# A forward transform folded twice over d in a fused spectral filter and MLP

## The chip, the cores and the metric

One core of a Trainium2 chip runs the kernel. The metric is device time in microseconds of one execution. The engines are TensorE (PE, matrix products; its weight loads are listed as PEld), VectorE (DVE), ScalarE (ACT), GpSimd (POOL) and SyncE (SP), whose queue issues most transfers.

## The reference

```python
def reference(A_x, A_w_r, A_w_i, B_x, B_w1, B_b1, B_w2, B_b2, gate_w):
    ...
        X = (lambda x, axes=(-2,-1): jnp.fft.rfft2(x, axes=axes))(x, axes=(-2, -1))
        W = w_r + 1j * w_i
        X = X * W
        y = (lambda x, s, axes=(-2,-1): jnp.fft.irfft2(x, s=s, axes=axes))(X, (S, D), axes=(-2, -1))
    ...
        h = jnp.einsum("bsd,df->bsf", x, w1) + b1
        h = _gelu(h)
        return jnp.einsum("bsf,fd->bsd", h, w2) + b2
    x = A_x
    g = _sigmoid((x * gate_w).sum(-1, keepdims=True))
    a = _A_ref(x, A_w_r, A_w_i)
    b = _B_ref(x, B_w1, B_b1, B_w2, B_b2)
    return g * a + (1 - g) * b
```

There are S = 2048 tokens of D = 512 elements and F = 1792 hidden units, all float32. Every token is Fourier transformed over d (257 frequencies remain) and the sequence over its 2048 positions, the result is multiplied by a complex filter and transformed back. An MLP with gelu works on the same tokens, and a gate per token mixes both.

## The kernel before

**Precision.** Products run on float32r operands, which keep 12 bits of mantissa here. So each operand x is split into h (ScalarE copies x into a float32r tile) and l = x - h (VectorE), and a full product is made of three: h times h, l times h, h times l. Tables are split on the host.

**Tiling.** Token s is 16a + j: 16 groups j of 128 tokens a. `forward(j)` (L546) transforms group j. It loads the group as four parts of 128 rows of d, folds the parts once (L551: `eo` is the sum and the difference of the upper and the lower half), splits `eo` into h and l, and multiplies with the table `cft` of cosines and sines into `pd` (one half for each of real and imaginary part, c = 0, 1). `high` (L569) makes eight products of 258 columns, two parts q, two values of c and the table's h and l; `low` (L575) makes four with the low part of the tokens. The 258 columns are 257 frequencies and one for the gate's logit. The second part of the table is made on the chip by copying and negating the first (L489 to L503). From `pd` ScalarE makes the high part `x{j}h`, VectorE the low part `x{j}l` and the logit; six products with the table `tf` transform over the 128 tokens (`py`), and L609 to L621 bring the two results into `Y[j]`: for the groups in `BY_ACT` with one VectorE instruction and two half-height ScalarE copies, for the first four groups with two half-height VectorE instructions.

After the forward transforms VectorE works through the rest of the sequence transform: `stage1`, a correction of two rows that goes through memory (`own_rows`), `filt`, `stage4`, and `inverse(c, h)`, which needs TensorE again (`pz`, `pa`).

**The MLP.** The hidden units come in two halves of seven tiles of 128, the tokens in four blocks c of 512. `mlp(half, c)` (L895) makes for each hidden tile f an up-projection of 12 products of 512 columns (`ph`), gelu on ScalarE, the split into `g` (h on ScalarE, l on VectorE), and then for four output tiles q down-projections of three products per hidden tile (`po`). The block's tokens are the pair `X[half, c]`; for block 0 they are split from the groups that the forward transform loads anyway, for the others `load_mx` (L532) loads and splits four groups, and `keep_x` (L524) stores the pair to memory for the second half. `load_w` (L884) loads a weight tile and splits it; for the second half the low part is made by `minus` (L447): ScalarE writes -h, and an accumulating transfer issued by POOL adds x from memory.

**What sets the order.** The functions only register steps with an engine, a modelled cost, a rank and the buffers they read and write. `Graph.schedule` (L211) simulates the engines and issues, on each engine, the ready step of the lowest rank whose buffers are to be had; a step waits for a slot of its buffer's tag (`slots`, L348, with limits for single classes in `most`, L352). The real engines then keep that order. Ranks: 0 for the transform's steps behind `pd`, `EARLY` 0.5, `FEED` 1 for the folds and most splits, `BULK` 5 for the stages behind the forward transform.

Of the kernel before, what the change touches and what calls it, by code (L numbers as in the profile page):

```python
# [14 lines left out]
ALU = mybir.AluOpType  # L15
# [11 lines left out]
CW = 272  # L27


FORD = np.concatenate([np.arange(0, HD, 2), np.arange(1, HD, 2), [HD]])  # L30
# [23 lines left out]
def _tables():  # L54

    d = np.arange(P)[:, None] + 0.5
    f = np.arange(NE)[None, :]
    th = 2 * np.pi * f * d / D
    cf = np.stack([np.cos(th), -np.sin(th)])
    cf[0][:, HD:] = 0.0  # L60
    cf[1][:, 0] = 0.0
    cf[1][:, HD + 1:] = 0.0
    cf = cf[:, :, FORD]

    cf = np.stack(_split(cf[:, :, :ND])).transpose(1, 2, 0, 3)
    cf = np.concatenate([cf, np.zeros((2, P, 2, CW - ND), np.float32)], 3)
# [8 lines left out]
    ])  # L75
# [89 lines left out]
class Graph:  # L165
# [45 lines left out]
    def schedule(self):  # L211
# [45 lines left out]
        while True:  # L257
            for e in list(ready):
                while ready[e] and busy.get(e, 0.0) <= now:
# [37 lines left out]
                    own = [q for q in s.after if q.eng == e == "pe"]  # L297
                    if own:
                        s.after = [q for q in s.after if q.eng != "pe"]
                        n += 1  # L300
                        heapq.heappush(events, (busy[e], n, own))
# [33 lines left out]
def tile_kernel(ctx: ExitStack, tc: tile.TileContext, xt, w1, w2, b1, b2, x0g, wf, wrev, out, consts):  # L335
# [15 lines left out]
    whole = ("xr", "wra", "wrb", "e2", "z", "ttab", "xhl", "wa", "wb", "hid", "so", "ba", "ctab", "gb")  # L351
    most = {("pm", "ph"): 2, ("pm", "po"): 2, ("pm", "po0"): 1, ("pm", "py"): 3, ("t2k", "pq"): 2}  # L352
# [11 lines left out]
    FEED, BULK, EARLY = 1, 5, 0.5  # L364

# [23 lines left out]
    def acc(dst, src, kb, reads, writes, rank=FEED):  # L389

        return add("pool", 2 * kb / 340, 3.6, lambda: nc.gpsimd.dma_start(dst(), src(), accum_op=ALU.add), reads, writes, rank)  # L391
# [19 lines left out]
    gs = one("gs", [P, 2, 2], parts=2)  # L411

    cft = buf("ctab", [P, 2, 2, 2, CW], F32R, "cf", parts=12)
    cfp = {(0, 0): (0,), (1, 0): (1,), (0, 1): (2, 3, 4), (1, 1): (5, 6, 7)}

    def cf(c, q):
        return cft.ap()[:, c, q]

    def cf_of(*cq):
        return [(cft, p) for k in cq for p in cfp[k]] + [(cft, g) for g in range(8, 12)]  # L420
# [7 lines left out]
    gb = one("gb", [P, 4, 4 * P], parts=4)  # L428
# [24 lines left out]
    def load_x(j, tag):  # L453
        x = buf("xr", [P, NQ, P], F32, f"x{tag}{j}")
        dma(lambda: sp.dma_start(x.ap(), xt[j]), 256, [], [x], j / 100 if tag == "f" and j in NORD[:4] else FEED)
        return x
# [14 lines left out]
    x0 = buf("z", [P, NQ + 1, P], F32, "xf0")  # L471
    XF = {0: x0}
    dma_act(lambda: act.dma_start(x0.ap().rearrange("p a b -> p (a b)")[:, :NQ * P + NQ], x0g), 258, [], [x0])
    for j in NORD[1:4]:
        XF[j] = load_x(j, "f")
    for c in range(2):
        dma(lambda c=c: raw(cf(c, 0), cf_d[c]), 272, [], [(cft, k) for k in (c, 8 + c, 10 + c)], 0.6)
# [5 lines left out]
    for k, op in enumerate((ALU.add, ALU.subtract)):  # L483
        tiny(lambda k=k, op=op: vec.tensor_tensor(gs.ap()[:, k], x0.ap()[:, NQ, 0:2], x0.ap()[:, NQ, 2:4], op=op), [x0],
             [(gs, k)])
    gcol = [lambda k=k: cft.ap()[:, :, :, k, NE - 1] for k in range(2)]
    tiny(lambda: vec.tensor_copy(gcol[0](), gs.ap()), [gs], [(cft, 8), (cft, 9)])
    tiny(lambda: vec.tensor_tensor(gcol[1](), gs.ap(), gcol[0](), op=ALU.subtract), [gs, (cft, 8), (cft, 9)], [(cft, 10), (cft, 11)])
    for c in range(2):  # L489
# [602 lines left out]
```

## Time and profile before

| | before |
|---|---|
| median of 3 runs | 380.79 us (380.64 to 381.64) |
| the profiled execution's own time | 381.64 us |
| its span, first to last instruction | 379.6 us |
| HBM read, written | 40.73 MB, 16.92 MB |

The profile's page gives for each engine the time in which it was busy and the number of its instructions. Rows of groups read: line, engine, operation, output<-input with shapes, count, then busy microseconds and mean nanoseconds of one, then the idle time before them and what ended it. Rows of the timeline read: start, length, engine, line, operation; where a row stands for several instructions, its length runs from the first start to the last end. Records of adjacent instructions on one engine overlap at their ends.

### The profile page before, as it was taken

How to read it: one execution, taken by the hardware profiler on the slowest of the kernel's cores; microseconds unless marked ns; L12 is line 12 of the kernel's file. 1: busy time of each engine (PE TensorE's matmuls, PEld its weight loads, DVE VectorE, ACT ScalarE, POOL GpSimd, SP SyncE). 2: the span in 40 equal slices, each digit the busy share in tenths (PEclk: the TensorE clock that was granted, in tenths of full speed). 3: DMA queues.
4: the chain of work that ended last, by engine and by line, in shares of the span. 5: the costliest groups of instructions: out<-in, count | busy, mean ns of one | idle time of the engine just before them, and what ended most of it. 6: DMA issues, size and time to landing. Idle time of an engine off the chain costs nothing.

```text
span 379.6 us, 5546 instructions
## 1 busy us (share of the span) xinstructions
PE 374.2 (99%) x1903; PEld 319.2 (84%) x1903; DVE 324.8 (86%) x683; ACT 220.7 (58%) x385; POOL 19.6 (5%) x26
## 2 busy tenths in 40 slices
PE   8999999989999999999999999999999999999996
PEld 7889999878888888888888888888888888888886
DVE  4999999879797999999999677967799799998732
ACT  6967678947622452288159984398429995134400
POOL 0000000000000000023022001100010000000000
PEclk9999999999999999999999999999999999999999
DMA  8975569895198006179568535413431129623031
GB/s 283 335 229 193 160 228 301 261 329 163 48 289 264 32 28 166 57 185 249 127 170 205 138 148 96 57 35 140 131 38 25 35 88 316 204 82 110 1 112 55
DMA packets 45172, 58.02 MB, mean 153 GB/s; under 512 B 4208, under 2 KB 27312, under 8 KB 44368
## 3 DMA queue, kind: packets, MB, share of 16 engines
q1 hardware_dynamic: 41832, 51.63, 41.9%
q0 software_dynamic: 3168, 5.77, 10.0%
q8 instruction: 15, 0.25, 0.3%
q10 hardware_dynamic: 144, 0.26, 0.2%
q14 instruction: 13, 0.11, 0.1%
HBM read 40.73 MB, written 16.92 MB: 152 GB/s over the span
## 4 chain that ended last, share of the span: by engine, by line
PE 94%; DMA 2%; ACT 1%; DVE 1%; issue 0%; SPq 0%
PE ph L400 40%; PE po L400 38%; PE pd L400 5%; PE pz L400 4%; PE pa L400 3%; PE py L400 3%; DMA wf<-in_wf 2%; PE none L400 1%; ACT y L616 0%; ACT pys L609 0%; SPq L397 0%; DVE pys L613 0%; ACT mxh L520 0%; DVE mxl L521 0%; ACT o L966 0%
## 5 line engine op out<-in xcount | busy, mean ns | idle before, releaser
L929 ACT ACTIVATE ph<-ph,b1t 128x512 f32<-128x512 f32 x56 | 37.0, 661 | 36.9 <-PE ph L400 36.4
L966 ACT ACTIVATE o<-po,b2t 128x512 f32<-128x512 f32 x16 | 11.1, 691 | 36.4 <-PE po L400 35.0
L801 ACT ACTIVATE sw<-y,al 64x512 f32<-64x512 f32 x32 | 23.2, 726 | 2.3 <-DVE y L664 1.6
L760 DVE TENSOR_TENSOR m<-y,wf 128x514 f32<-128x514 f32 x32 | 21.2, 692 | 0.1
L400 PE MATMUL pd<-cf,eoh 128*128 128x258 f32 x128 | 17.8, 282 | 0.0
L400 PEld LDWEIGHTS pd<-cf,eoh 128*128 128x128 f32 x128 | 16.8, 190 | 0.4
L808 DVE SCALAR_TENSOR_TENSOR pq<-y,al,sw 128x256 f32<-128x256 f32 x32 | 14.3, 481 | 1.4 <-ACT sw L804 1.4
L794 ACT ACTIVATE tg<-ti 128x128 fp32r<-128x128 f32 x16 | 5.0, 312 | 15.5 <-DVE ti L792 14.0
L986 DVE TENSOR_TENSOR o<-y,po 128x256 f32<-128x256 f32 x8 | 3.1, 419 | 10.8 <-PE po L400 10.8
L552 DVE TENSOR_TENSOR eo<-xf 128x256 f32<-128x256 f32 x32 | 12.3, 420 | 0.0
L391 POOL DMA_DIRECT2D bacc<-o x8 | 7.0, 873 | 97.2 <-ACT o L969 97.2
L559 DVE TENSOR_TENSOR eol<-eo,eoh 128x512 fp32r<-128x512 f32 (+1 forms) x17 | 11.0, 654 | 0.2
L616 ACT ACTIVATE y<-pys 64x257 f32<-64x257 f32 x24 | 10.1, 420 | 1.9 <-DVE pys L613 1.6
L557 ACT ACTIVATE eoh<-eo 128x512 fp32r<-128x512 f32 (+1 forms) x17 | 10.1, 603 | 1.5 <-DVE eo L552 1.5
L804 ACT ACTIVATE sw<-y 1x512 f32<-1x512 f32 x16 | 10.1, 631 | 0.4
L969 ACT ACTIVATE o<-po 128x512 f32<-128x512 f32 x8 | 4.8, 601 | 9.4 <-PE po L400 5.2
L400 PE MATMUL pd<-cf,eol 128*128 128x258 f32 x64 | 10.1, 283 | 0.0
L391 POOL DMA_DIRECT2D wa7l<-in_w x1 | 1.0, 1017 | 163.1 <-PE ph L400 163.1
L400 PEld LDWEIGHTS pd<-cf,eol 128*128 128x128 f32 x64 | 8.9, 190 | 0.3
L609 ACT ACTIVATE pys<-py 128x257 f32<-128x257 f32 x16 | 6.2, 386 | 5.0 <-PE py L400 4.6
L860 DVE TENSOR_TENSOR u<-pa,od 128x512 f32<-128x512 f32 x8 | 5.5, 690 | 3.4 <-ACT od L850 3.2
L521 DVE TENSOR_TENSOR mxl<-xm,mxh 128x512 fp32r<-128x512 f32 x12 | 7.9, 687 | 0.5 <-ACT mxh L520 0.4
(688 smaller groups left out, 1322.0 us busy)
## 6 DMA issues: line engine op xcount, KB each, us to landing
wf<-in_wf SPq DMA_DIRECT2D x16, 257.0 KB, 4.1
tf<-tf SPq DMA_DIRECT2D x16, 256.0 KB, 3.1
bacc<-o SPq DMA_DIRECT2D x16, 256.0 KB, 3.5
xf<-in_xt SPq DMA_DIRECT2D x15, 256.0 KB, 2.7
war<-in_w SPq DMA_DIRECT2D x14, 256.0 KB, 4.0
wbr<-in_w SPq DMA_DIRECT2D x14, 256.0 KB, 3.3
xm<-in_xt SPq DMA_DIRECT2D x12, 256.0 KB, 4.1
bb<-bacc SPq DMA_DIRECT2D x8, 256.0 KB, 4.0
```

The source lines that it names most:

```text
L391: return add("pool", 2 * kb / 340, 3.6, lambda: nc.gpsimd.dma_start(dst(), src(), accum_op=ALU.add), reads, writes, rank)
L400: pe.matmul(ps, w, x, start=start, stop=stop)
L552: v(lambda s=s, op=op: vec.tensor_tensor(eo.ap()[:, s], x.ap()[:, 0:2], x.ap()[:, 2:4], op=op), 256, [x], [(eo, s)], FEED)
L557: a(lambda k=k: act.activation(h.ap()[:, k], eo.ap()[:, k], AF.Copy), 256 * len(ps), sub[0], sub[1], FEED)
L559: v(lambda k=k: vec.tensor_tensor(l.ap()[:, k], eo.ap()[:, k], h.ap()[:, k], op=ALU.subtract), 256 * len(ps), sub[0] + sub[1], sub[2], FEED)
L616: a(lambda o=o, i=i: act.activation(Y[j].ap()[o:o + HP, 1], pys.ap()[i:i + HP, 1], AF.Copy), 257, [(pys, 1)], [(Y[j], 1 + k)], 0, more=0.1)
L760: v(lambda mk=mk, k=k, y=y, w=w: vec.tensor_tensor(mk.ap(), y.ap(), w.ap()[:, k:k + 1, :ND].to_broadcast([P, 2, ND]), op=ALU.mult), 514, [ ...
L801: a(lambda sw=sw, y=y, o=o, i=i: act.activation(sw.ap()[o:o + HP], y.ap()[i:i + HP, ::-1, :HD], AF.Copy, scale=al.ap()[i:i + HP, 0:1]), 51 ...
L804: a(lambda sw=sw, y=y, j=j: act.activation(sw.ap()[HP:HP + 1], y.ap()[HP:HP + 1, ::-1, :HD], AF.Copy, scale=math.cos(math.pi * j / NJ)), 5 ...
L808: v(lambda sw=sw, pq_=pq_, y=y, j=j, k=k, op=op: vec.scalar_tensor_tensor(pq_.ap()[:, k], y.ap()[:, k, :HD], al.ap()[:, 1 + j:2 + j], sw.a ...
L929: a(lambda f=f, ps=ps: act.activation(ps.ap(), ps.ap(), AF.Gelu_apprx_tanh, bias=b1t.ap()[:, f:f + 1]), 600, [b1t], [ps], 0.9 if half else ...
L966: a(lambda o=o, ps=ps, q=q: act.activation(o.ap(), ps.ap(), AF.Identity, bias=b2t.ap()[:, q:q + 1]), 600, [b2t, ps], [o])
```

## The change

**The fold.** `forward` folds a second time: `w` is the sum and the difference of the two parts of each half of `eo`. The parts are taken in an order on the host that makes odd and even frequencies each depend on one fold alone, so each (c, s) has one product over 128 rows. The table holds h and l side by side (576 columns in place of two parts of 2 x 272), so one product of 258 or 254 columns gives token-high times both; the low part of the tokens is multiplied with table-high alone, 130 columns. The table's columns for some even frequencies (0, 64, 128, 192) are rounded to values that need no low part, which the inverse table's factors undo. The two column blocks of `pd` are added afterwards: ScalarE reads the high block in one instruction for each c, VectorE subtracts in one for each c, and two more VectorE instructions add the block of the table's low part. The table's second half is no longer made on the chip.

**Staging.** `BY_ACT` holds all 16 groups. The folds and their loads get ranks 0.80 to 0.95 by their turn (`turn_of`); the weights and block 1's tokens get ranks between them. Tokens of blocks 1 to 3 come from a copy `xc` laid out by part, one part of four groups at a time. The first half's down-projection weights and the hidden tiles of block 0 get their low part by -h on ScalarE and an accumulating transfer on POOL; for the latter gelu's output goes to `gst` in SBUF first. All weights and their raw loads share 29 buffers (33 before), the token pairs have four buffers in place of two and share them with `gb` and `bb`, and `x{j}h`, `x{j}l` have two fixed pairs. In the planner, a step on VectorE or ScalarE frees its followers on the same engine when it ends, and the cost of an accumulating transfer is booked as 2.3 x KB/340 and 3.4 us in place of 2 x KB/340 and 3.6.

```diff
-FORD = np.concatenate([np.arange(0, HD, 2), np.arange(1, HD, 2), [HD]])
+TE, TW = 320, 576
+EXACT = [0, 64, 128, 192]
+NX = len(EXACT)
+FORD = np.concatenate([np.arange(1, HD, 2), EXACT, [f for f in range(0, HD, 2) if f not in EXACT], [HD]])
...
-                    own = [q for q in s.after if q.eng == e == "pe"]
+                    own = [q for q in s.after if q.eng == e in ("pe", "vec", "act")]
...
-    slots = {"xr": 3, "wra": 3, "wrb": 2, "t2k": 7, "e2": 4, "z": 4, "ttab": 3, "xhl": 2, "wa": 2 * FA, "wb": 2 * FA, "hid": 2 * FA,
-             "so": 2, "ba": 2, "bb": 1, "pf": 2, "pm": 4, "ti": 1}
+    slots = {"xr": 3, "t2k": 7, "e2": 4, "ttab": 3, "xhl": 4, "w": 29, "hid": 2 * FA,
+             "so": 2, "ba": 2, "bb": 1, "gst": 2, "xm": 1, "pf": 2, "pm": 4, "ti": 1}
...
+    def turn_of(n):
+        return 0.8 + 0.01 * n
...
+    def pair():
+        turn[0] += 1
+        return zb[turn[0] % 2 * 2:][:2]
...
-            for j1 in range(4):
-                split_1(X[0, c], load_x(c + 4 * j1, "m"), j1)
+            for q in range(NQ):
...
+                x = buf("xm", [P, 4 * P], F32, f"xm{c}{q}")
+                dma(lambda q=q, x=x: sp.dma_start(x.ap(), xc[c, q]), 256, [], [x], turn_of(8+0.5*q - 2) if c == 1 else FEED)
+                a(lambda part=part, x=x: act.activation(part(h), x.ap(), AF.Copy), 512, [x], [(h, q)], turn_of(8+0.5*q) if c == 1 else FEED)
...
     def forward(j):
+        feed = turn_of(NORD.index(j))
...
+        for s, op in enumerate(ops):
+            v(lambda s=s, op=op: vec.tensor_tensor(w.ap()[:, s], eo.ap()[:, :, 0], eo.ap()[:, :, 1], op=op), 256, [eo],
+              [(w, s)], feed)
...
+        odd, even = (slice(0, 2 * P + 2), slice(0, 2 * P + 2)), (slice(2 * P + 2, 4 * P), slice(TE, TE + 4 * P - 2 * P - 2))
+        odd_l, even_l = (slice(P, 2 * P + 2),) * 2, (slice(2 * P + 2, 3 * P + 4), slice(TE, TE + P + 2))
+
+        def high(ss=(0, 1), cs=(0, 1)):
+            for s in ss:
                 for c in cs:
-                    mm(ps.ap()[:, c, :NE], h.ap()[:, c, q], cf(c, q)[:, 0, :NE], q == 0, False)
-                    mm(ps.ap()[:, c, :NE], h.ap()[:, c, q], cf(c, q)[:, 1, :NE], False, False)
+                    o, i = odd if s != c else even
+                    mm(ps.ap()[:, c, o], h.ap()[:, s, c], cft.ap()[:, c, i], s == 0, False)
         def low():
             for c in range(2):
-                for q in range(2):
-                    mm(ps.ap()[:, c, :NE], l.ap()[:, c, q], cf(c, q)[:, 0, :NE], False, q == 1)
+                for s in range(2):
+                    o, i = odd_l if s != c else even_l
+                    mm(ps.ap()[:, c, o], l.ap()[:, s, c], cft.ap()[:, c, i], False, s == 1)
...
-            m(high, NE, 8, [h, cft], [ps], 0)
-        m(low, NE, 4, [l, cft], [ps], 0)
...
+            m(high, NE, 4, [h, cft], [ps], 0)
+        m(low, 236, 4, [l, cft], [ps], 0)
+        xh, xl = pair()
...
+        for c in range(2):
+            a(lambda c=c: act.activation(segs(xh, c, 0, P + c), segs(ps, c, P, P + 4), AF.Copy), 256, [(ps, c)], [(xh, c)], 0)
+        for c in range(2):
+            v(lambda c=c: vec.tensor_tensor(segs(xl, c, 0, P + c), segs(ps, c, P, P + 4), segs(xh, c, 0, P + c), op=ALU.subtract),
+              256, [(ps, c), (xh, c)], [(xl, c)], 0)
+        for o, i in ((slice(0, P), slice(0, P)), (slice(P + NX, 2 * P), slice(3 * P + NX, 4 * P))):
+            v(lambda o=o, i=i: vec.tensor_tensor(xl.ap()[:, :, o], xl.ap()[:, :, o], ps.ap()[:, :, i], op=ALU.add), 256, [ps],
+              [xl], 0)
...
-    def early(n, f, rank):
-        return EARLY + 0.05 if n == "b" else EARLY if f else rank
+    def early(n, f):
+        return turn_of(8+0.5*f if n == "b" else f-1) if f or n == "b" else EARLY
...
+        if f < FA and (n == "a" or f < 0):
+            v(lambda: vec.tensor_tensor(l.ap(), t.ap(), h.ap(), op=ALU.subtract), 512, [t, h], [l], rank)
+        else:
+            minus(h, l, lambda b: b.ap(), 512, lambda: src, ([h], [l]), rank)
...
+            if half == c == 0:
+                t = buf("gst", [P, 512], F32, f"gs{c}_{f}")
+                h, l = G[f] = [buf("hid", [P, 512], F32R, f"g{c}_{f}{k}") for k in "hl"]
...
+                a(lambda t=t, h=h: act.activation(h.ap(), t.ap(), AF.Copy), 512, [t], [h], rank)
+                a(lambda h=h, l=l: act.activation(l.ap(), h.ap().bitcast(F32), AF.Copy, scale=-1.0), 512, [h], [l], rank)
+                acc(lambda l=l: l.ap(), lambda t=t: t.ap(), 256, [t], [l], rank)
+                continue
...
-    BY_ACT = NORD[4:]
+    BY_ACT = NORD[0:]
```

More of the change, by code (lines that the diff above doesn't have):

```diff
@@ L334, in tile_kernel @@
 @with_exitstack
-def tile_kernel(ctx: ExitStack, tc: tile.TileContext, xt, w1, w2, b1, b2, x0g, wf, wrev, out, consts):
+def tile_kernel(ctx: ExitStack, tc: tile.TileContext, xt, xc, w1, w2, b1, b2, x0g, wf, wrev, out, consts):
     nc = tc.nc
@@ L454, in load_x @@
         x = buf("xr", [P, NQ, P], F32, f"x{tag}{j}")
[L455 removed]
+        dma(lambda: sp.dma_start(x.ap(), xt[j]), 256, [], [x], j / 100 if j in NORD[:4] else turn_of(NORD.index(j) - 2))
         return x
@@ L834, in part @@
         def part(p, z, k, first, last):
-            for ft in (1, 0):
-                mm(ps.ap()[:, ft, k], CI[0].ap()[:, k, p, ft], z.ap()[:, ft, k].rearrange("p a b -> p (a b)"), first, last)
+            for ft in range(2):
+                mm(ps.ap()[:, 1 - ft, k], CI[0].ap()[:, k, p, ft], z.ap()[:, ft, k].rearrange("p a b -> p (a b)"), first, last)
         def high(k):
@@ L900, in mlp @@
         G = {}
+        if half and c == 2:
+            bb2 = buf("xhl", [P, NQ, 4 * P], F32, "bb2", parts=NQ, cls="bb")
         for f in fs:
```

175 lines of the change are left out of this document (97 added, 78 removed).

## The prediction

> **What bounds the kernel now.** I read the page's busy shares first, then the busy times by stretch, then the chain that ended last, then single instructions.
>
> ```profile
> span 379.6 us, 5546 instructions
> PE 374.2 (99%) x1903; PEld 319.2 (84%) x1903; DVE 324.8 (86%) x683; ACT 220.7 (58%) x385; POOL 19.6 (5%) x26
> ...
> PE 94%; DMA 2%; ACT 1%; DVE 1%; issue 0%; SPq 0%
> ```
>
> TensorE is busy 374.2 of 379.6 us and holds 94% of the chain. What is taken from TensorE's work comes off the end, as long as TensorE always has something to do. The stretches (columns: span, then busy time and instruction count of PE, PEld, DVE, ACT, POOL, then clock, DMA share, GB/s) say how near that limit is:
>
> ```profile
> 0.00:12.00 12.00, 10.95 (x49) 9.22 (x50) 7.10 (x19) 8.07 (x15) 0.20 (x4) 1.00 0.88 305
> 12.00:72.00 60.00, 60.00 (x396) 54.94 (x395) 56.95 (x137) 46.95 (x95) 0.00 (x0) 1.00 0.74 238
> 72.00:80.00 8.00, 8.00 (x40) 6.67 (x38) 5.66 (x12) 6.15 (x11) 0.00 (x0) 1.00 0.94 286
> 80.00:120.00 40.00, 38.94 (x173) 31.91 (x172) 34.66 (x64) 18.37 (x29) 0.00 (x0) 1.00 0.71 213
> 120.00:200.00 80.00, 80.00 (x355) 66.24 (x354) 78.24 (x164) 39.21 (x66) 8.88 (x10) 1.00 0.50 129
> 200.00:280.00 80.00, 80.00 (x405) 67.96 (x404) 63.18 (x134) 54.18 (x93) 8.74 (x10) 1.00 0.45 111
> 280.00:340.00 60.00, 60.00 (x308) 51.20 (x307) 56.93 (x116) 38.31 (x65) 1.73 (x2) 1.00 0.40 120
> ```
>
> The forward transforms fill 12 to 75 us. There VectorE has 56.95 of 60 us: it is as full as TensorE. The clock is 1.00 throughout. The only wait of TensorE after its first instruction is at 80 us, where block 1 of the MLP starts and the low part of its tokens is late:
>
> ```profile
> 79.74 0.19 PEld L400 LDWEIGHTS ph<-mxh,wa0h 128*128 128x128 f32 x1
> 79.96 0.39 PE L400 MATMUL ph<-mxh,wa0h 128*128 128x512 f32 x1
> ...
> 81.41 0.19 PEld L400 LDWEIGHTS ph<-mxl,wa0h 128*128 128x128 f32 x1 [1.48 <-DVE mxl L521]
> 81.41 0.50 PE L400 MATMUL ph<-mxl,wa0h 128*128 128x512 f32 x1 [1.06 <-DVE mxl L521]
> 81.52 0.19 PEld L400 LDWEIGHTS ph<-mxh,wa0l 128*128 128x128 f32 x1
> ```
>
> **TensorE's share of the change.** Of 12 products of 258 columns per token group, 4 of 258 or 254 columns and 4 of 130 remain. The chain in order of time (start, length, what) prices the wide one; the last row prices 512 columns:
>
> ```profile
> 24.98 0.95 PE pd L400 x8
> ...
> 31.09 2.75 PE ph L400 x12
> ...
> 61.42 1.92 PE pd L400 x16
> ...
> 317.09 9.55 PE po L400 x42
> ```
>
> 1.92/16 = 0.120 us for 258 columns; 192 of them are 23.0 us. 9.55/42 = 0.227 us for 512, so a column costs (0.227 - 0.120)/254 = 0.42 ns. No row is narrower than 256. If columns alone counted, 130 would cost 0.120 - 128 x 0.00042 = 0.066 us; at the other end a narrow product costs as much as a wide one, 0.120. Every product also loads a full 128x128 weight tile. After the wait at 81.41 nothing holds the loads back, and the second starts 0.11 us after the first. A product that streams faster than its successor's weights arrive waits for them. So I take 0.11 us, which also is near what the changed code books for it (236 columns at a 2400th of a us each plus 0.0135, 0.112). After: 64 x 0.120 + 64 x 0.11 = 14.7 us. **TensorE saves 8.3 us**; the ends are 7.7 (narrow as wide) and 11.1 (columns alone, 64 x 0.066 = 4.2).
>
> The Trainium skill, page TensorE: Matmul & The Clock Gate, section Back-to-back issue gap, gives a sustained 81 ns for a load and product of 128 columns; by it the 64 narrow ones would be 5.2 us and the saving 10.1. Its section on LDWEIGHTS gives columns/1.2 ns, 107 ns for 128; the 0.11 us above agrees with that one, and no run here yet shows 81.
>
> **VectorE's share.** Adjacent instructions overlap at their ends, so I count steps, not records:
>
> ```profile
> 13.38 0.76 DVE L552 TENSOR_TENSOR eo<-xf 128x256 f32<-128x256 f32 x2
> ...
> 104.15 1.89 DVE L521 TENSOR_TENSOR mxl<-xm,mxh 128x512 fp32r<-128x512 f32 x3
> ...
> 61.86 0.42 DVE L610 TENSOR_TENSOR y<-py,pys 128x257 f32<-128x257 f32 x1
> 62.20 0.42 DVE L613 TENSOR_TENSOR pys<-py,pys 128x257 f32<-128x257 f32 x1
> 62.64 0.70 DVE L590 TENSOR_TENSOR x3l<-pd,x3h 128x516 fp32r<-128x516 f32 x1
> 63.25 0.15 DVE L592 TENSOR_REDUCE logit<-pd 128x1 f32<-128x2 f32 x1
> ...
> 11.34 0.29 DVE L493 CAST cf<-cf 128x256 fp32r<-128x256 f32 x1
> ```
>
> 256 elements: 0.76 - 0.42 = 0.34 us. 512: (1.89 - 0.69)/2 = 0.60. 516: 63.25 - 62.64 = 0.61. Each group gains two second folds (0.68), reads the low half in two instructions instead of one (0.68 - 0.61 = 0.07) and adds two table-low columns into it (0.68): 1.43 x 16 = 22.9 us. Off go 14 splits of 512 (wb of the first half and the hidden tiles of block 0, 8.4 us), one of three output instructions for four groups (4 x 0.34 = 1.4) and the table's two copies (0.6). **Net 12.5 us more VectorE**, nearly all before 90 us. The new strided reads of PSUM have no row; I price them as the plain ones, and their upper end is in the slower rival.
>
> **The other engines.** ScalarE gains 14 negated copies (0.6 each, 8.4), eight half-height moves, and one more read of PSUM per group:
>
> ```profile
> L616 ACT ACTIVATE y<-pys 64x257 f32<-64x257 f32 x24 | 10.1, 420 | 1.9 <-DVE pys L613 1.6
> L609 ACT ACTIVATE pys<-py 128x257 f32<-128x257 f32 x16 | 6.2, 386 | 5.0 <-PE py L400 4.6
> L443 ACT ACTIVATE g_1h<-ph 128x512 fp32r<-128x512 f32 x2 | 1.2, 601 | 0.1
> L497 ACT ACTIVATE cf<-cf 128x256 fp32r<-128x256 f32 x2 | 0.8, 413 | 0.6 <-DMA cf<-cf 0.6
> 0.00:100.00 100.00, 97.89 (x564) 86.17 (x565) 88.93 (x200) 73.83 (x139) 0.20 (x4) 1.00 0.75 239
> ```
>
> 8.4 + 8 x 0.42 + 16 x (2 x 0.386 - 0.601) - 0.8 for the table's negation = 13.7 us, onto 73.8 in the first 100: under 88. It costs nothing while VectorE, fuller still, paces the phase; without that cover it would be late itself once it needs 12 us more. The 14 accumulating transfers are new in this phase:
>
> ```profile
> q0 software_dynamic: 3168, 5.77, 10.0%
> ...
> wa8l<-in_w POOLq DMA_DIRECT2D x1, 256.0 KB, 4.9
> ...
> wb8l<-in_w POOLq DMA_DIRECT2D x1, 256.0 KB, 5.5
> ...
> 45.04 0.40 PE L400 MATMUL po<-g_6h,wb6h 128*128 128x512 f32 x1
> ```
>
> 10% of 379.6 us for 22 transfers is 1.73 us of all 16 queues each, 24 us in all, onto a share of 0.74 (44 of 60 us). The stores of the token copies are ranked behind and give way. A low part then lands about 5 us after its issue (rows from HBM; from SBUF there is none, and I take the same). Hidden tile 6 is first used at 45.0 us, 11.2 us after its up-projection ended (31.09 + 2.75 = 33.8), so the 7 us of negation and transfer are covered. POOL's queue holds nothing else then. The second half's weights now share 29 buffers with their raw loads; each up-projection group (12 products, 2.72 us) frees two, and 19 us of down-projection lie between the frees and the next use, so I cost this at nothing. So with xs, gb and bb sharing four token buffers: block c+1's low part waits for block c's stores as before, behind 19 us of down-projection.
>
> **The sum.** The profiled execution took 381.64 us (2.04 around its span), 0.85 above the median of 380.79. 381.64 - 8.3 = 373.3, and on the median 372.5. I keep 1.1 us for a wait like the one at 80 us: the tokens of block 1 come earlier, but there are more places for such a wait. Without it and with the saving at 11.1: 380.79 - 12.2 = **368.6, the low end**.
>
> **The rivals.** TensorE's saved 8.3 us and VectorE's added 12.5 pull apart by 20.8 us. Where that lands decides.
>
> *Columns alone* (nothing but the price of the narrow product is different): 380.79 - 11.1 = 369.7. Against it stands the 0.11 us between loads.
>
> *VectorE is late at the end.* The work from stage 1 to the last inverse starts 12.5 us later. Its last output transfer now is issued here:
>
> ```profile
> L874 SPq DMA_DIRECT2D out<-w x8: 372/474/513, 312.4 to 361.6; - x8
> ...
> out<-w SPq DMA_DIRECT2D x8, 256.0 KB, 3.9
> ```
>
> 361.6 + 12.5 + 0.5 + 3.9 = 378.5 against a TensorE-bound end of span of 379.6 - 8.3 = 371.3. With nothing absorbed the median is 380.79 - 1.1 = 379.7. To vanish, 7.2 us must go into VectorE's idle time, which from 12 to 340 us is 3.1 + 2.3 + 5.3 + 1.8 + 16.8 + 3.1 = 32 us, half of it inside the inverses of 200 to 280 us, where each waits on its own chain. If about half of 7.2 is found: 376.
>
> *TensorE starves in the forward phase: the slower one.* The last forward group is done on VectorE at 75 us now (the row of 74.73 below), so near 87 after. TensorE reaches block 1 at 79.96 - 8.3 = 71.7. It needs 15 us of block 1 to bridge. A group of 12 products is 2.72 us, and two fit into PSUM before VectorE must split a hidden tile, at rank 1, behind every fold (0.80 to 0.95). If VectorE never gets to these splits, 5.4 us are filled and 9.9 are lost: 372.5 + 9.9 = 382.4, and 387.8 if block 1's tokens are late too. It decides from three groups down: three leave a loss of 7 us, no gain. For it: VectorE at 95%. Against it: even now VectorE finds time between folds for work of the lowest rank:
>
> ```profile
> 63.31 0.69 DVE L662 TENSOR_TENSOR a0d<-y 128x514 f32<-128x514 f32 x1
> ...
> 66.38 0.69 DVE L662 TENSOR_TENSOR a0d<-y 128x514 f32<-128x514 f32 x1
> ...
> 74.73 0.43 DVE L610 TENSOR_TENSOR y<-py,pys 128x257 f32<-128x257 f32 x1 [0.24 <-ACT pys L609]
> ```
>
> Stage 1 runs there while groups 7 and 11 still are under way, because the folds wait for buffers. The same gaps serve the splits.
>
> **How the numbers follow.** A measurement of this kernel tells about 0.3% (1.1 us) from no change. Forecast 0.55 (369.5 to 375.5), columns alone 0.07, late VectorE 0.18 (375 to 380), starved TensorE 0.20 (380 to 388). Predicted time 372.5. Faster: 0.55 + 0.07 + 0.15 of the late case = 0.77, less 0.02 for prices without a row: 0.75. Same: 0.05, the ends of the two last cases. Slower: 0.20. The range is 368.6 to 382.4; beyond it lie the worse half of starvation and little below.
>
> **What would show it.** Narrow products at 0.11 us start to start (0.066 would be columns alone); 64 + 64 products writing pd, about 14.7 us; VectorE near 337 us; up-projections of block 1 between the last forward products, without gaps on TensorE, and ScalarE under 90 of the first 100 us. The last inverse's transfer near 365 us or before proves the work absorbed; after 372 it is the late case. I am wrong if TensorE shows more than 4 us of idle time before its last product, or if pd takes over 20 us.

## The result and the profile after

| | before | after |
|---|---|---|
| median of 6 runs each, same chip | 380.72 us (380.3 to 381.73) | 390.51 us (388.37 to 391.24) |
| span of the profiled execution | 379.6 us | 389.4 us |
| ratio after to before | | 1.0244 (95%: 1.0214 to 1.0275) |

The change makes the kernel 2.4% slower; 372.5 us was forecast. The page of the kernel after, at the lines shown of before:

```profile
span 389.4 us, 5547 instructions
...
PE 374.5 (96%) x1839; PEld 311.6 (80%) x1839; DVE 340.5 (87%) x743; ACT 229.8 (59%) x421; POOL 32.3 (8%) x52
...
PE 38%; DVE 30%; ACT 19%; DMA 8%; issue 4%; SPq 0%; DVEq 0%; ACTq 0%
```

TensorE executes 64 products fewer and is listed as busy as long as before (374.5 against 374.2 us): the records of its products have grown longer, and part of the time that is lost lies inside them. Its share of the chain that ended last fell from 94% to 38%; VectorE (30%), ScalarE (19%) and transfers (8%) now stand in it too. The stretches of after (columns as before):

```profile
0.00:12.00 12.00, 9.27 (x40) 7.71 (x41) 6.17 (x19) 5.95 (x11) 0.67 (x16) 1.00 0.85 298
12.00:72.00 60.00, 55.81 (x308) 46.78 (x307) 56.66 (x159) 51.89 (x115) 12.38 (x14) 1.00 0.98 264
72.00:80.00 8.00, 8.00 (x47) 6.98 (x46) 7.47 (x21) 5.58 (x14) 0.00 (x0) 1.00 1.08 358
80.00:120.00 40.00, 40.00 (x193) 33.51 (x192) 38.09 (x76) 26.63 (x47) 0.00 (x0) 1.00 0.63 201
120.00:200.00 80.00, 80.00 (x355) 66.26 (x354) 77.93 (x160) 36.82 (x61) 6.96 (x8) 1.00 0.53 148
200.00:280.00 80.00, 78.00 (x380) 63.17 (x379) 63.95 (x133) 53.40 (x92) 9.65 (x11) 1.00 0.50 119
280.00:340.00 60.00, 59.24 (x296) 49.73 (x295) 52.35 (x106) 35.73 (x60) 2.63 (x3) 1.00 0.43 115
```

TensorE is idle in the first 72 us, where but for its start it was not, and again behind 200 us. Between 72 and 200 us it has no gap at all. VectorE is no fuller from 12 to 72 us than before (56.66 against 56.95).

Busy time hides part of this, so I added up starts: what lies between the start of a product and the start of the next, beyond 0.120 us for 254 to 258 columns, 0.227 for 512 and 0.11 for 130, is lost time. Shorter distances are not set off against it, and the 12 products ahead of the real work are left out.

| | work of the products | lost before 110 us | lost after 110 us | lost in all |
|---|---|---|---|---|
| before | 367.3 us | 2.7 | 1.2 | 3.9 us |
| after | 359.0 us | 12.5 | 9.5 | 22.0 us |

Work fell by 8.3 us and lost time rose by 18.1: 9.8 us more, and the spans differ by 9.8. The fold's saving is there and is spent twice over on waits. The timeline of TensorE in the kernel after shows the narrow product and two waits (start, length, then what):

```profile
21.17 0.63 PE L419 MATMUL py<-zb,tf 128*128 128x258 f32 x3 [0.75 <-ACT pys L666]
...
37.59 1.06 PE L419 MATMUL py<-zb,tf 128*128 128x258 f32 x4 [1.05 <-DVE pys L670]
...
56.42 0.56 PE L419 MATMUL pd<-cf,eol 128*128 128x130 f32 x4
56.82 0.44 PE L419 MATMUL po<-g_4h,wb4h 128*128 128x512 f32 x1
```

Four products of 130 columns take 0.40 us here; over all 64 the median from start to start is 0.112 us. Whom TensorE waits for in the whole run (total, times, longest):

```profile
PE pz L419 <- DVE zb L887: 2.2, 2, 1.6
PE pd L419 <- ACT eoh L598: 1.7, 1, 1.7
PE py L419 <- ACT pys L666: 1.2, 2, 0.7
...
PE py L419 <- DVE pys L670: 1.1, 1, 1.1
PE po L419 <- DVE g_12l L467: 0.6, 1, 0.6
```

No single wait is large, and no engine or tile owns them. They stand at many small hand-overs.

### The profile page after: what moved, and what is told of

Same layout as the page of the kernel before. It is cut to its first block, busy times and chain, and to the rows that moved or that the text cites. A ratio compares the mean times of both kernels' runs of the same rounds, so it can differ in the third digit from the quotient of the medians.

```text
span 389.4 us, 5547 instructions
## 1 busy us (share of the span) xinstructions
PE 374.5 (96%) x1839; PEld 311.6 (80%) x1839; DVE 340.5 (87%) x743; ACT 229.8 (59%) x421; POOL 32.3 (8%) x52
## 3 DMA queue, kind: packets, MB, share of 16 engines
q0 software_dynamic: 5184, 9.44, 15.7%
## 4 chain that ended last, share of the span: by engine, by line
PE 38%; DVE 30%; ACT 19%; DMA 8%; issue 4%; SPq 0%; DVEq 0%; ACTq 0%
PE po L419 20%; PE ph L419 12%; ACT sw L858 4%; DVE m L817 4%; DMA wf<-in_wf 2%; DVE y L721 2%; ACT ph L1003 2%; PE pa L419 2%; DMA bb<-bacc 2%; PE pd L419 2%; ACT sw L861 2%; ACT y L673 2%; DMA ti<-ti 1%; PE pz L419 1%; PE py L419 1%
## 5 line engine op out<-in xcount | busy, mean ns | idle before, releaser
L419 PE MATMUL py<-zb,tf 128*128 128x258 f32 x96 | 17.7, 297 | 3.3 <-ACT pys L666 1.2
L419 PEld LDWEIGHTS py<-zb,tf 128*128 128x128 f32 x96 | 14.3, 189 | 6.5 <-ACT pys L666 1.8
L419 PEld LDWEIGHTS pa<-zb,ci 128*128 128x128 f32 x96 | 13.2, 189 | 2.8 <-ACT zb L884 1.6
L419 PE MATMUL pa<-zb,ci 128*128 128x256 f32 x96 | 14.4, 286 | 0.3 <-ACT zb L884 0.2
L642 DVE TENSOR_TENSOR zb<-pd,zb 128x256 fp32r<-128x256 f32 x32 | 12.1, 419 | 2.3 <-ACT zb L640 1.9
L885 DVE TENSOR_TENSOR zb<-pz,zb 128x512 fp32r<-128x512 f32 x16 | 11.0, 685 | 3.0 <-ACT zb L884 3.0
L593 DVE TENSOR_TENSOR w<-eo 128x256 f32<-128x256 f32 x32 | 12.8, 419 | 0.3
L590 DVE TENSOR_TENSOR eo<-xf 128x256 f32<-128x256 f32 x32 | 12.3, 419 | 0.0
L646 DVE TENSOR_TENSOR zb<-zb,pd 128x256 fp32r<-128x256 f32 (+1 forms) x32 | 11.9, 412 | 0.4
L600 DVE TENSOR_TENSOR eol<-w,eoh 128x512 fp32r<-128x512 f32 (+1 forms) x17 | 11.1, 655 | 1.0 <-ACT eoh L598 1.0
L887 DVE TENSOR_TENSOR zb<-zb,pz 128x512 fp32r<-128x512 f32 x16 | 11.0, 686 | 0.4
```

The source lines that it names most:

```text
L419: pe.matmul(ps, w, x, start=start, stop=stop)
L590: v(lambda s=s, op=op: vec.tensor_tensor(eo.ap()[:, s], x.ap()[:, 0:2], x.ap()[:, 2:4], op=op), 256, [x], [(eo, s)], feed)
L593: v(lambda s=s, op=op: vec.tensor_tensor(w.ap()[:, s], eo.ap()[:, :, 0], eo.ap()[:, :, 1], op=op), 256, [eo], [(w, s)], feed)
L600: v(lambda k=k: vec.tensor_tensor(l.ap()[:, k], w.ap()[:, k], h.ap()[:, k], op=ALU.subtract), 256 * len(ps), sub[0] + sub[1], sub[2], feed)
L642: v(lambda c=c: vec.tensor_tensor(segs(xl, c, 0, P + c), segs(ps, c, P, P + 4), segs(xh, c, 0, P + c), op=ALU.subtract), 256, [(ps, c), (x ...
L646: v(lambda o=o, i=i: vec.tensor_tensor(xl.ap()[:, :, o], xl.ap()[:, :, o], ps.ap()[:, :, i], op=ALU.add), 256, [ps], [xl], 0)
```

## The experiments

**Three loads, each lightened with the order kept.** First I asked which added load makes TensorE wait. In each of three kernels every instruction stays at its place, and one kind is made short. The 32 adds of the table-low block handle 4 of 128 columns, so most of that sum is left out:

```diff
-            v(lambda o=o, i=i: vec.tensor_tensor(xl.ap()[:, :, o], ...
+            v(lambda o=slice(o.start, o.start + 4), i=slice(i.start, i.start + 4): vec.tensor_tensor(xl.ap()[:, :, o], ...
```

> The changed kernel with its order of instructions kept; the 32 VectorE instructions that add the table's low block run over 4 columns in place of 128 (so that part of the sum is left out). That takes about 32 x 0.26 = 8 us off VectorE before 90 us and nothing off any other engine. Theory V (VectorE is full, and its lateness is what TensorE waits for, early and at the end): the time falls by 5 us or more from 390.5, to 385 or below. Theory D (the 14 accumulating transfers fill the DMA queues and everything lands late): less than 2 us. Theory A (ScalarE is full from 10 to 55 us): less than 2 us.

The 14 new accumulating transfers move 2 of 512 columns, so the rest of those low parts stays at -h:

```diff
-        acc(lambda: view(l), src, 256, [], rest[1], rank)
+        acc((lambda: view(l)[:, :2]) if few else (lambda: view(l)), (lambda: src()[:, :2]) if few else src, 256, ...
...
-                acc(lambda l=l: l.ap(), lambda t=t: t.ap(), 256, [t], [l], rank)
+                acc(lambda l=l: l.ap()[:, :2], lambda t=t: t.ap()[:, :2], 256, [t], [l], rank)
```

> The changed kernel with its order kept; the 14 accumulating transfers of the forward phase move 2 of 512 columns (so those low parts stay minus the high part). That takes about 24 us of all 16 queues out of the first 75 us. Theory D: the time falls by 5 us or more. Theories V and A: less than 2 us, since no engine loses work.

The 14 new negations on ScalarE write 16 of 512 columns, and POOL clears the rest ahead of its transfer, so most of those low parts lacks the -h:

```diff
-                a(lambda h=h, l=l: act.activation(l.ap(), h.ap().bitcast(F32), AF.Copy, scale=-1.0), ...
+                a(lambda h=h, l=l: act.activation(l.ap()[:, :16], h.ap()[:, :16].bitcast(F32), AF.Copy, scale=-1.0), ...
```

> The changed kernel with its order kept; the 14 negations of the forward phase on ScalarE write 16 of 512 columns, and POOL, which is idle, clears the rest (so those low parts come out wrong). ScalarE loses about 14 x 0.5 = 7 us before 55 us. Theory A: the time falls by 4 us or more. Theories V and D: less than 2 us.

| run | median | ratio to before (95%) |
|---|---|---|
| short adds | 389.28 us | 1.0207 (1.0187 to 1.0228) |
| small accumulates | 389.72 us | 1.0220 (1.0194 to 1.0247) |
| short negations | 389.56 us | 1.0202 (1.0180 to 1.0224) |

All three stay within 0.5% of the changed kernel's ratio (1.0244). The page and the stretch from 12 to 72 us of the run with short adds:

```profile
PE 373.7 (96%) x1839; PEld 311.7 (80%) x1839; DVE 333.5 (86%) x743; ACT 230.2 (59%) x421; POOL 32.3 (8%) x52
```

```profile
12.00:72.00 60.00, 55.92 (x308) 47.38 (x308) 51.27 (x158) 52.37 (x116) 12.37 (x14) 0.98 0.99 264
```

VectorE has 5.4 us less to do there (51.27 against 56.66), and TensorE's busy time is the same. (The clock of 0.98 is told at the end; the two executions at a mean of 0.999 took 388.67 and 389.01 us.) None of the three theories of a load holds: with this order, less of one kind of work doesn't feed TensorE. (The three together weren't lightened.)

**The fold alone.** The fold was put on the staging, the ranks and the planner's rules of before, and planned anew (the reverse of the diff's parts outside `forward`, `_tables` and the pairs):

```diff
-    slots = {"xr": 3, "t2k": 7, "e2": 4, "ttab": 3, "xhl": 4, "w": 29, "hid": 2 * FA,
+    slots = {"xr": 3, "wra": 3, "wrb": 2, "t2k": 7, "e2": 4, "ttab": 3, "xhl": 2, "wa": 2 * FA, "wb": 2 * FA, "hid": 2 * FA,
...
-        feed = turn_of(NORD.index(j))
+        feed = FEED
...
-    BY_ACT = NORD[0:]
+    BY_ACT = NORD[4:]
```

> The second fold on the staging of before (own weight buffers and VectorE splits, two token buffers, ranks, first four groups without the ScalarE copies), planned anew. VectorE then has 22 us more than before in the forward phase and block 1 can't start early. If the staging costs the time: 373 to 382. If the fold's VectorE work costs it and the staging was there to hide it: slower than the changed kernel, 393 to 402, with TensorE idle between 50 and 100 us.

It took 403.7 us, 1.058 (1.0563 to 1.0598), 1.7 us beyond the slower of the two ranges expected. TensorE loses 34.2 us, 33.2 of them before 110 us. So the fold without its staging is far worse, and staging, ranks and rules together win 13 us of it back. The stretch that shows it:

```profile
72.00:120.00 48.00, 38.81 (x152) 32.44 (x152) 42.51 (x102) 29.68 (x59) 0.00 (x0) 0.68 0.68 200
```

The granted clock is 0.68 there, so part of the loss is the clock's; that is told at the end.

**What the planner believed.** The planner is part of the kernel: it simulates the engines and fixes their order, and its simulated end can be set against the span on the chip. For the kernel before it said 380.2 us (chip 379.6). For the changed one it said 377.8, and the chip took 389.4. It thus believed in a gain of 2.4 us, though 8.3 us of work are gone: some 6 us of new waits stood in the order as planned. And the chip ran 11.7 us late against it (377.75 to two places). The changed follower rule is a candidate: it lets a follower on VectorE or ScalarE start the moment the booked cost of its predecessor is over. The timeline of VectorE in the kernel after shows what the chip does:

```profile
210.36 0.68 DVE L717 TENSOR_TENSOR c3s<-y 128x512 f32<-128x512 f32 x1
211.08 0.69 DVE L717 TENSOR_TENSOR y<-c3s,c3s 128x512 f32<-128x512 f32 x1
211.69 0.69 DVE L719 TENSOR_TENSOR y<-c3s,c3s 128x512 f32<-128x512 f32 x1
212.29 0.42 DVE L721 SCALAR_TENSOR_TENSOR d1u<-y 128x256 f32<-128x256 f32 x1
```

The second line reads what the first wrote: 0.72 us from start to start. The third reads the same input as the second and needs nothing of it: 0.61. A dependent instruction costs some 0.11 us more. The rule of before left 0.12 us there and so put other work between; the new one does not. Counted in the issued orders, an instruction stands right behind the one on VectorE that the planner makes it wait for 34 times before and 167 times after.

Not each of these pairs costs the time, because the planner also counts two that write different columns of one buffer. The same timeline, a little earlier:

```profile
206.47 0.43 DVE L819 TENSOR_TENSOR y<-m,m 128x257 f32<-128x257 f32 x1
206.81 0.42 DVE L821 TENSOR_TENSOR y<-m,m 128x257 f32<-128x257 f32 x1
207.15 0.68 DVE L467 TENSOR_TENSOR g_8l<-ph,g_8h 128x512 fp32r<-128x512 f32 x1
```

L821 writes the other half of `y` and starts 0.34 us after L819, as early as the independent third starts after it. Where a pair is delayed, the second record begins some 0.03 us behind the end of the first; elsewhere the two overlap by 0.08. By that sign 14 of the 34 pairs are delayed before and 89 of the 167 after.

Four kernels test it. The changed kernel with the old rule on both engines:

```diff
-                    own = [q for q in s.after if q.eng == e in ("pe", "vec", "act")]
+                    own = [q for q in s.after if q.eng == e == "pe"]
                     if own:
-                        s.after = [q for q in s.after if q.eng != e]
+                        s.after = [q for q in s.after if q.eng != "pe"]
```

> The changed kernel, planned again with the follower rule of the kernel before: an instruction of VectorE or ScalarE that needs the result of another one of the same engine is booked 0.12 or 0.18 us after that one's end, and only TensorE's followers start at once. All computation is the same; the order is another. The plan's own span is 384.9 us (changed kernel 377.8, kernel before 380.2, its trace 379.6). Theory P (the plan's rule: dependent pairs are placed back to back, each runs about 0.12 us later on the chip, and the delays add up because VectorE has no slack): the chip now follows the plan, 384 to 388 us, so faster than the changed kernel's 389.5 to 390.5 by 2 to 6 although its plan is 7 us longer, and TensorE is less than 3 us behind the plan at 200 us. Theory Q (the plan underprices the changed kernel's load, transfers above all, whatever the rule): the chip stays 11 to 12 us behind the plan, 396 to 398.

With the new rule on TensorE and ScalarE alone, then on TensorE and VectorE alone:

```diff
-                    own = [q for q in s.after if q.eng == e in ("pe", "vec", "act")]
+                    own = [q for q in s.after if q.eng == e in ("pe", "act")]
```

> The changed kernel, planned again with the changed follower rule for TensorE and ScalarE, and the rule of the kernel before for VectorE. Plan 380.8 us. Running this order again on paper with 0.12 us (VectorE) and 0.18 us (ScalarE) behind every dependency within an engine gives 382.3. Theory P: 382 to 385 us. If ScalarE's followers were as harmful as VectorE's: near 390. Theory Q: 391 to 393.

```diff
-                    own = [q for q in s.after if q.eng == e in ("pe", "vec", "act")]
+                    own = [q for q in s.after if q.eng == e in ("pe", "vec")]
```

> The changed kernel, planned again with the changed follower rule for TensorE and VectorE, and the rule of the kernel before for ScalarE. Plan 383.6 us, shorter than that of the run with the old rule on both (384.9). The order run again on paper with 0.12 us behind VectorE's dependencies gives 394.8. Theory P: 392 to 397 us, 8 to 12 us longer than the run with the old rule on both. Theory Q: 395 to 396 as well, but then the run with the old rule on both is near 397, and this one is not slower than it.

And the kernel before with nothing changed but the rule:

```diff
-                    own = [q for q in s.after if q.eng == e == "pe"]
+                    own = [q for q in s.after if q.eng == e in ("pe", "vec", "act")]
                     if own:
-                        s.after = [q for q in s.after if q.eng != "pe"]
+                        s.after = [q for q in s.after if q.eng != e]
```

> The kernel before, planned again with the changed follower rule alone: no fold, no new staging, the same work. Its plan is 392.8 us (380.2 with its own rule: its ranks were set for that one), and run again on paper with the delays 401.5. The kernel before with its own rule runs 0.6 us under its plan. Theory P: 398 to 403 us, some 6 to 10 above its plan. Theory Q, in which only the changed kernel's load is underpriced: 392 to 394, as planned.

| kernel | rule on VectorE | dependent neighbours on VectorE by the planner (delayed in the trace) | planned end | span on the chip | chip less plan | median, ratio to before (95%) |
|---|---|---|---|---|---|---|
| before | old | 34 (14) | 380.2 | 379.6 | -0.6 | 380.72 |
| after | new | 167 (89) | 377.75 | 389.4 | +11.7 | 390.51, 1.0244 (1.0214 to 1.0275) |
| after, old rule | old | 71 (40) | 384.9 | 385.7 | +0.8 | 387.1, 1.0146 (1.0110 to 1.0181) |
| after, new on ScalarE | old | 63 (37) | 380.8 | 385.2 | +4.4 | 387.26, 1.0149 (1.0116 to 1.0182) |
| after, new on VectorE | new | 179 (95) | 383.6 | 395.9 | +12.3 | 396.19, 1.0387 (1.0325 to 1.0450) |
| before, new rule | new | 135 (69) | 392.8 | 400.5 | +7.7 | 402.44, 1.0551 (1.0533 to 1.0570) |

Where VectorE's followers are booked without a delay, the chip ends 8 to 12 us behind the plan, with the fold and without it; where they are booked with it, it ends between 0.6 us ahead and 4.4 behind. The theory that the changed kernel's load is underpriced whatever the rule expected 396 to 398 for the first run and 392 to 394 for the last, and both fell. Although its planned end is 7 us later, the changed kernel with the old rule is 3 us faster than the changed kernel. One expectation was missed: with ScalarE alone on the new rule 382 to 385 us was expected and 387.26 came, which points to ScalarE's followers not being free either. The sizes of the last two rows aren't of one cause: there the clock stood at half for some 14 and 17 us as well (below). TensorE was busy for 12.4 and 14.3 us of that, so up to 6 and 7 us of these rows can be the clock's. The rule's part rests on the rows without that: the changed kernel had the full clock and ended 11.7 us late, and with the old rule it ended 0.8 late although 6.8 us at half clock lie in that run.

The delays do not make up the whole 11.7 us. 75 more of 0.117 us are 8.8 us on VectorE, and not each reaches the end. As an estimate I ran the changed kernel's order again on paper at its planned costs: with the 89 delays that the trace shows it ends at 381.9 us in place of 377.8, and with 0.10 us for each of ScalarE's 69 dependent neighbours (0.656 us from start to start for 512 columns, 0.558 for independent ones) at 384.0. That is about half of the 11.7 us; what makes up the rest isn't shown.

Putting the rule right gives back about 3 of the 9.8 us, though. The late waits are gone (lost after 110 us: 0.9 in place of 9.5), but before 110 us TensorE now loses 17.6, 3.9 of them from 44 to 53 us, where the clock fell to half.

**Other orders of the same work.** Is the rest the order's, or can no order feed TensorE? I drew ranks and margins at random, kept what came out shorter with 0.12 to 0.15 us behind each dependency on VectorE and ScalarE, and ran three results. The first changes no instruction (beside these lines, other ranks and one booked delay differ):

```diff
-SPARE = 0.4
+SPARE = 0.11352387536479619
-AHEAD = {"vec": 0.35, "act": 0.35}
+AHEAD = {"vec": 0.08888414214838125, "act": 0.021912708774442447}
...
-                    own = [q for q in s.after if q.eng == e in ("pe", "vec", "act")]
+                    own = [q for q in s.after if q.eng == e == "pe"]
...
-        return turn_of(8+0.5*f if n == "b" else f-1) if f or n == "b" else EARLY
+        return turn_of(3.0603185796219385+0.46958285965552715*f if n == "b" else 0.0610785657611681*f+0.37695227163908296) if f or n == "b" else EARLY
```

> The changed kernel with every instruction and transfer it has, in another order: the follower rule of the kernel before, and other ranks and margins for the planner (weights of the first half, block 1's tokens, table and token loads, spare time ahead of a product), drawn at random a few hundred times and kept when the order, run again on paper with 0.12 to 0.15 us behind a dependency within VectorE or ScalarE, came out shorter. That gives 376.7 us here, and 378.9 with transfers 0.3 to 0.7 us later than planned. Theory R (the loss that is left with the old rule, 387.1 us, is the order's): 378 to 382 us. Rival S (VectorE's and the queues' added work holds the forward phase back in any order): 384 us or more, whatever the paper says.

The other two also give VectorE some of its splits back. The second one:

```diff
-                    own = [q for q in s.after if q.eng == e in ("pe", "vec", "act")]
+                    own = [q for q in s.after if q.eng == e in ("pe", "act")]
...
-            if half == c == 0:
+            if half == c == 0 and 2 <= f < 6:
...
-    BY_ACT = NORD[0:]
+    BY_ACT = NORD[2:]
```

> As the run with another order alone, but the shares of the engines were searched too: of the 14 low parts that the changed kernel gets by a negated copy and an accumulating transfer, three hidden tiles (0, 1 and 6) go back to a split on VectorE, and two of the four token groups that ScalarE was given more of get the old form; the follower rule is the old one for VectorE, the changed one for ScalarE. On paper 375.1 us, 377.0 with transfers later, and no wait of TensorE of over 0.8 us. Theory R: 376 to 380. Rival S: 384 or more.

and the third:

```diff
-        if f < FA and (n == "a" or f < 0):
+        if f < FA and (n == "a" or f < 1):
...
-            if half == c == 0:
+            if half == c == 0 and 3 <= f < 5:
...
-    BY_ACT = NORD[0:]
+    BY_ACT = NORD[1:]
```

> A second order found in the same way: five hidden tiles of seven go back to a split on VectorE and one weight tile of the first half does, one token group gets the old form. On paper 374.2 us, 376.2 with transfers later. Theory R: 375 to 380. Rival S: 384 or more, and more than the run with fewer splits on VectorE.

As a control, the kernel before was searched in the same way, with its own work and rule (margins, ranks and one booked delay alone differ):

```diff
-AHEAD = {"vec": 0.35, "act": 0.35}
+AHEAD = {"vec": 0.47124965487382076, "act": 0.5840495322174006}
...
-            G[f] = split(f"g{c}_{f}", "hid", [P, 512], ps, lambda x: x, 512, 0.9 if half else FEED if c else EARLY)
+            G[f] = split(f"g{c}_{f}", "hid", [P, 512], ps, lambda x: x, 512, 0.7493237329552618 if half else FEED if c else EARLY)
```

> The kernel before with its own work and follower rule, and with the planner's ranks and margins drawn and kept in the same way as in the three searched orders of the changed kernel. On paper it comes to 379.0 us where the kernel before has 379.3: TensorE loses only 3.9 us between products there, so an order can win no more than that. Theory F (the 4 us by which the best searched order of the changed kernel beats the kernel before come from the fold, with an order that feeds TensorE): no difference to the kernel before, 380 to 382 us. Rival G (a search of orders wins as much without the fold): 377 to 378.

| kernel | dependent neighbours on VectorE by the planner (delayed in the trace) | lost before, after 110 us | span | median | ratio to before (95%) |
|---|---|---|---|---|---|
| after, other order | 21 (14) | 11.1, 3.1 | 381.6 | 383.27 us | 1.0063 (1.0037 to 1.0090) |
| after, order and shares, first | 20 (15) | 6.9, 1.8 | 376.4 | 378.83 us | 0.9942 (0.9924 to 0.9960) |
| after, order and shares, second | 15 (8) | 6.2, 1.8 | 375.4 | 377.11 us | 0.9888 (0.9867 to 0.9909) |
| before, searched | 35 (16) | 1.4, 1.2 | 378.5 | 380.73 us | 0.9971 (0.9951 to 0.9990) |

The last but one is the fastest kernel of this study, 1.1% faster than before, and its page and first stretches answer to those above:

```profile
span 375.4 us, 5535 instructions
...
PE 367.1 (98%) x1839; PEld 310.7 (83%) x1839; DVE 335.9 (89%) x750; ACT 226.2 (60%) x413; POOL 27.0 (7%) x46
```

```profile
0.00:12.00 12.00, 8.86 (x40) 7.09 (x41) 6.14 (x20) 5.84 (x11) 0.67 (x16) 1.00 0.81 271
12.00:72.00 60.00, 59.31 (x342) 51.53 (x340) 58.89 (x164) 49.34 (x109) 7.12 (x8) 1.00 0.94 276
```

TensorE has 59.31 us of the 60 in the forward phase, with VectorE at 58.89, fuller than in either kernel. So the theory that VectorE's added work holds the phase back in any order (384 us or more) is refuted. For the queues the evidence is weaker: this kernel has 8 of the 14 new accumulating transfers (POOL issues 46 in place of 52), and the run with another order, which has them all, came only just under 384. The span of the fastest kernel follows from the same account: 8.3 us of work saved, 4.1 more lost (8.0 against 3.9), 4.2 us gained, and the spans differ by 4.2. The search by itself brings 0.3% to the kernel before, so some 0.8% is the fold's, with the reservation that the shares of the engines were searched for the fold alone. The run with another order alone missed its expectation (378 to 382) by 1.3 us, and lost 4.6 us from 40 to 50 us, where the clock stood at half for 3.4 us. How much of the step from it to the two others is due to the splits that VectorE got back, and how much to a better order, wasn't separated.

## Why the prediction was wrong

**What failed** is one term of the sum: "I keep 1.1 us for a wait like the one at 80 us". TensorE's waits cost 18.1 us more than before. The forecast took it as given that the new order would keep TensorE fed, with VectorE's added 12.5 us put into gaps. It went through engines, queues and buffers, but it neither set the planner's own end beside its sum nor priced the rule by which the planner lets a follower start. Both spoke against it. The plan gains 2.4 us, not 8.3, so some 6 us of the new waits stood in the order as planned. And the chip, 0.6 us ahead of the old plan, ended 11.7 us behind the new one. The rule was named in the text of the change and has no price in the prediction: under the old booking 14 neighbours on VectorE are delayed, under the new one 89. By the estimate above the delays on VectorE and ScalarE make up about half of the 11.7 us; what makes up the other half, and why the order as planned held its 6 us, stays open. That 7 us of the miss are the order's and not the work's is shown: the same instructions in another order took 383.27 us, and 377.11 with a few splits moved between engines as well.

**TensorE's share: right.** The narrow product takes 0.112 us from start to start where 0.11 was taken; columns alone (0.066) is refuted. In the fastest kernel, where little waits, the 128 products on `pd` take 14.4 us from start to start (14.7 forecast, 23.0 before): 8.6 us saved where 8.3 was forecast. In the kernel after they take 15.9, waits included.

**VectorE's share: right in kind, too small.** 15.7 us more busy time, not 12.5. It was forecast before 90 us, but the first 100 us hold only 0.7 us more (89.59 against 88.93): the work slid behind, and the last forward group was done on VectorE at 92 us, not 87. But busy time wasn't what decided, as the short adds show. The order did, and the delay between dependents, which busy time doesn't hold, is part of it.

**ScalarE and the accumulating transfers at no cost: right.** Busy time on ScalarE rose by 9.1 us, 5.1 of them in the first 100 us (78.94 against 73.83), where 13.7 was forecast, and shortening the negations or the transfers moves the time by less than 0.5%, little more than the intervals can tell.

**Late VectorE** (376 to 379.7) foresaw lost time at the end but priced it from added work alone. The lost 9.5 us after 110 us are of this kind, and they vanish with the old rule (0.9) though the work is the same. The last inverse's transfer was issued at 371.5 us (361.6 before), just short of the 372 that was named as its sign.

**Starved TensorE in the forward phase** (382.4, or 387.8) had the right sign and the wrong place. It put the loss behind 72 us, where block 1 must bridge the last groups. There the trace of after has no gap: 8.00 of 8.00 and 40.00 of 40.00 us. The bridge worked as the argument against this rival said, and the loss came before it, at hand-overs such as `eoh` to `pd` and `pys` to `py`. Both rivals came true in part and at once, which the prediction didn't allow for, so 390.5 lies beyond every case and beyond the range.

**The named tests** decide it as they were meant to: more than 4 us of idle time before the last product was the sign of a wrong forecast. 14.9 us of the span are idle (389.4 - 374.5; before 379.6 - 374.2 = 5.4). Of these 3.7 lie behind the last product (before 3.3), so 11.2 stand where 2.1 stood. The 128 products on `pd` stayed under their limit of 20 us.

## What to carry to other kernels

Where a program plans the order, treat each change to its model as a change to every instruction, and set its planned end against the chip first: a plan that the chip meets within 1 us before and misses by 12 after says where to look. A saving on the engine that bounds is worth what the order leaves of it; here the same work took 390.5 or 383.3 us, and 377.1 with a few splits moved between engines. Shortening one instruction kind in a fixed order tells whether a load decides, and if nothing moves, look at the order.

## What the runs showed of the hardware

**A dependent neighbour on VectorE starts 0.11 us later** than an independent one (0.72 against 0.61 us, above). The Trainium skill, page VectorE: DVE Perf Modes, section The DRAIN you can't avoid, says of a chain of copies that a semaphore after each costs nothing extra. It does not speak of neighbours of which one reads what the other wrote, and these rows show that they cost 0.11 us.

**Behind waits of little over 1 us TensorE's clock stood at half for several us.** The timeline of TensorE in the changed kernel with the old rule:

```profile
44.34 0.48 PE L419 MATMUL py<-zb,tf 128*128 128x258 f32 x2 [1.12 <-ACT eoh L598]
...
45.58 0.58 PE L419 MATMUL py<-zb,tf 128*128 128x258 f32 x1 [0.28 <-DVE zb L646]
...
48.35 0.63 PE L419 MATMUL po<-g_2l,wb2h 128*128 128x512 f32 x1
48.78 0.63 PE L419 MATMUL po<-g_2h,wb2l 128*128 128x512 f32 x1
...
52.48 0.40 PE L419 MATMUL po<-g_3l,wb3h 128*128 128x512 f32 x1
52.72 0.40 PE L419 MATMUL po<-g_3h,wb3l 128*128 128x512 f32 x1
```

and its granted clock (the column ahead of the last two) in that stretch:

```profile
44.00:45.00 1.00, 0.66 (x5) 0.69 (x6) 0.97 (x4) 0.96 (x3) 0.34 (x1) 1.00 1.32 195
45.00:46.00 1.00, 0.72 (x4) 0.38 (x2) 1.00 (x4) 0.94 (x2) 0.00 (x0) 0.60 0.84 190
46.00:48.00 2.00, 1.91 (x9) 1.74 (x9) 1.81 (x5) 1.70 (x6) 0.86 (x1) 0.50 1.10 311
```

After 1.12 us without work and 0.28 more, products of 512 columns start 0.43 us apart in place of 0.24, until about 52 us: some 6.8 us at half speed, so about 3 us are lost beside the wait's own length, if the wait is the cause. The same stands in the kernel before with the new rule (behind a wait of 1.87 us at 225 us) and, over most of 65 to 107 us, in the fold alone (37.6 us, in which TensorE was busy for 28.0, so up to 14 us of that run). Not every such wait is followed by it: the changed kernel's 1.05 us ahead of 37.59 was not, while the same wait in the run with short negations (1.01 us ahead of 37.16) was, with a clock of 0.51 from 39 to 42 us. In the run with another order the longest wait shortly ahead of the fall was 0.72 us, and of its ten executions the three with a mean clock of 0.99 took 385.5 to 386.0 us, the others 382.1 to 383.3. That waits bring the fall about is thus argued from where it stands; what decides it isn't shown. The Trainium skill, page TensorE: Matmul & The Clock Gate, section Part 1: The HAM clock gate, has the clock fall after an idle window of about 3.4 us; here falls also stand behind far shorter idle time (1.12 us above). A planner that books such a wait at its own length can book it too low.
